# Block-sorted attention and a squared-ReLU MLP in one kernel: turning q, k and x^T on TensorE instead of by transposing transfers

## The chip, the cores and the metric

The kernel runs on one core of a Trainium2 chip. A core has a matrix engine (TensorE, PE in the profile, with its weight loads as PEld), three engines for elementwise work (VectorE or DVE, ScalarE or ACT, GpSimd or POOL), an engine that here only issues transfers (SyncE or SP), and sixteen DMA engines. PE reads from the on-chip memory (SBUF) and writes into PSUM, from where DVE or ACT copies results back. The metric is the device time of one execution in microseconds; the median of several runs counts.

## The reference

Four batches of eight heads, 768 positions, head size 64. A sort matrix of 8x8 for each head is normalised five times by rows and columns and then mixes the eight blocks of 96 positions of k and of v. Each block of q attends to the mixed block of the same number. The result, as x of 3072 tokens by 512, goes through an MLP of width 2048.

```python
    for _ in range(5):
        P = P - np.max(P, axis=-1, keepdims=True)
        P = np.exp(P)
        P = P / (np.sum(P, axis=-1, keepdims=True) + 1e-09)
        P = P / (np.sum(P, axis=-2, keepdims=True) + 1e-09)
    k_sorted = np.einsum('bhij,bhjcd->bhicd', P, k_b).reshape(B, H, S, D)
    v_sorted = np.einsum('bhij,bhjcd->bhicd', P, v_b).reshape(B, H, S, D)
    scores = scale * np.matmul(q_b, k_sb.transpose(0, 1, 2, 4, 3))
    attn = np.exp(scores)
    attn = attn / (np.sum(attn, axis=-1, keepdims=True) + 1e-09)
    # per token, x = attn @ v_sb with the heads side by side
    h = np.maximum(x @ w_in, 0.0)
    return (h * h @ w_out).astype(np.float32)
```

## The kernel before

Work is cut into units of a batch and a pair of heads (`Unit`). A unit needs q turned (head size on the partitions), k sorted and turned, v sorted, the scores (`s_sc`, L684), their exponentials (L704, L713), the product with v (`s_av`, L875), the division (L885, L886), and the turn of the result into x^T (`s_xt`), from which the MLP reads. The MLP (`ffn_unit`) goes in eight groups of 384 tokens: 16 x 4 up matmuls (L997, `hp`) with a relu on ACT (L1005) and a square on DVE (L1008) for each of the 16 tiles, and then three times 16 down matmuls (L1027, `op`; the last tile in two parts, L1055), copied out and stored.

Order. Every step is first recorded as an operation with an engine, a cost and its dependencies. A planner (`Plan.run`) then lays them out. PE has two queues, attention and MLP. Attention operations stand in an order given by the table `DUES`: a number for each step says after how many MLP chunks it is due. `FIRST` is the order written out by hand for the first half of batch 0, with which the kernel starts. `Ring` keeps track of who uses which buffer. Batch 0 is worked off in two halves, before and beside the first MLP groups; batches 1, 2 and 3 are hidden between the MLP groups of the batch before.

How q, k and x^T are turned before the change:

- Batch 0: `s_q` turns q on PE with an identity matrix (L563), `s_sort` and `s_sort2` (L613, L649) multiply k and v by an expanded sort matrix `w_all`, which sorts and turns in one step.
- Batch 1, the first two head pairs: the same steps, in `sort_second`.
- Batch 1, the other two, and batches 2 and 3 (ten units): k is sorted in its own layout by `s_nat` (L769, tiles of 32x32 of PE's array, stage "N"), copied to `kn`, and then `s_turn` (stage "Z") issues a transposing transfer on SP (`k_turn`, L824) into `kx`, which DVE copies into blocks (L829). For q, DVE gathers a pair (`q_pair`, L841) and a second transposing transfer turns it (`q_turn`, L851).
- v of batches 1 to 3 goes by `s_nat` too, and then to DRAM and back in blocks (`v_way`, L793, L799).
- x^T: `s_xt` issues a transposing transfer (L910) for the second half of batch 0, for batches 2 and 3 and for three pairs of batch 1; the rest is turned on PE (L928).

A `gate` on POOL (L390) keeps the early transposing transfers of x^T and the last q load of batch 1 behind a weight load. POOL's `hold` (L1144) lets the loads of batches 2 and 3 start only when x^T of the batch before is there.

While PE has nothing to do before the MLP starts, `fill` (L440) runs matmuls of ones into a PSUM tile. `Ring.idle` chooses the tile: one in which no recorded operation runs during the gap.

The first two pairs of q are loaded in float32 and cast by ACT (L460), after the second and third exponential of the sort matrix.

Of the kernel before, what the change touches and what calls it, by code (L numbers as in the profile page):

```python
# [21 lines left out]
    (0, "K"): (-265.0, -237.0, -495.0, -419.0),  # L22
    (0, "S"): (-232.5, -234.0, -349.0, -310.0),
    (0, "T"): (-184.0, -236.0, -400.0, -291.5),
    (0, "A"): (-135.0, -150.0, -300.0, -111.0),
    (0, "X"): (-58.0, -109.0, -251.5, -80.5),
    (0, "W"): (-267.0,),
    (1, "V"): (-117.0, -62.5),
    (1, "Q"): (-58.5,),
    (1, "N"): (None, -31.0),  # L30
    (1, "Z"): (None, None, 2.5, 48.5),
    (1, "S"): (-45.5, -5.0, 5.0, 50.0),
    (1, "A"): (-27.0, -4.5, 31.5, 51.5),
    (1, "X"): (40.0, 23.5, 37.0, 53.5),
    (2, "L"): (40.0,),
    (2, "N"): (75.5, 79.0),
    (2, "V"): (60.5, 82.5),
    (2, "Z"): (81.0, 82.5, 94.0, 83.5),
    (2, "S"): (86.0, 86.5, 96.0, 93.5),
    (2, "A"): (86.0, 88.0, 99.0, 94.5),  # L40
    (2, "X"): (97.5, 103.0, 103.0, 102.0),
    (3, "L"): (109.0,),
    (3, "N"): (111.5, 130.0),
    (3, "V"): (112.5, 144.0),
    (3, "Z"): (128.5, 139.0, 153.0, 149.0),
    (3, "S"): (144.0, 153.0, 158.0, 153.5),
    (3, "A"): (145.0, 153.5, 159.5, 154.5),
    (3, "X"): (150.5, 170.0, 236.5, 211.5),
# [4 lines left out]
FIRST = ("K0' v0 K1 v1 S0 t0' S1 t1' A0 K2' V2 A1 K3 S2 t2 v3 S3 x1' A2 T3' x0' A3 X2' F0 F1 F3 "  # L53
         "F4 F6 F7 X3")
# [18 lines left out]
class Ring:  # L73


    def __init__(self, n):
        self.users = [[] for _ in range(n)]
        self.all = [[] for _ in range(n)]
        self.turn = -1
        self.pinned = set()  # L80
        self.holders = [None] * n

    def take(self, pin=False):
        assert len(self.pinned) < len(self.users)
        self.turn = (self.turn + 1) % len(self.users)
        while self.turn in self.pinned:
            self.turn = (self.turn + 1) % len(self.users)
        if pin:
            self.pinned.add(self.turn)
        old = self.users[self.turn]  # L90
        self.users[self.turn] = []
        slot = Slot(self.turn)
        self.holders[self.turn] = slot
        return slot, old

    def use(self, slot, *ops):
        assert self.holders[slot] is slot, "taken again before its last use"
        self.users[slot] += ops
        self.all[slot] += ops

    def idle(self, t0, t1):

        for slot, ops in enumerate(self.all):
            if all(op.end <= t0 or op.begin >= t1 for op in ops):
                return slot
# [79 lines left out]
def kernel(  # L185
# [48 lines left out]
    rkx, rkn, rqi, rqz = Ring(3), Ring(4), Ring(4), Ring(6)  # L234
# [43 lines left out]
    kvT_r, et_r, vs_r, qz_r = [], [], [], []  # L278
    for n in range(3):
        sT = const.tile([128, 2, S + 32], BF16, name=f"kvT{n}")  # L280
        for x in (HS, S):
            nc.vector.memset(sT[:, :, x:x + 32], 0.0)
        kvT_r.append(sT)
        qz = const.tile([128, 2, NA, 128], BF16, name=f"qz{n}")
        qz_r.append(qz)
        vs = (qz.rearrange("p h a x -> p (h a x)")[0:96, 0:NB * 2 * 66]
              .rearrange("p (n h x) -> p n h x", n=NB, h=2))
# [13 lines left out]
    kn_r = [const.tile([128, NA, 2, D], BF16, name=f"kn{n}") for n in range(4)]  # L301
    qi_r = [const.tile([128, NA, 2, D], BF16, name=f"qi{n}") for n in range(4)]
    kx_r = []
    for n in range(3):
        kx_r.append(const.tile([128, 128 * NA], BF16, name=f"kx{n}"))
# [8 lines left out]
    w_all = const.tile([128, H + HP, NB, C0], BF16)  # L314
# [22 lines left out]
    def in_tiles(b, t, h0):  # L337
        return b > 1 and t > 0 or b == 1 and t == 2 or b == 1 and t == 1 and h0 == HP
# [44 lines left out]
    def loads_after(deps):  # L383
# [5 lines left out]
        def gate(e):  # L389
            nc.gpsimd.tensor_copy(out=xT[0:1, 0:HP - 1, HS:HS + 1],  # L390
                                  in_=w_out_bf[0:1, NT // 2 - HP + 1:NT // 2, 0:1])

        for t, g in ((2, 0), (2, 1), (1, 0), (0, 0), (1, 1), (0, 1)):
            if t == 0 and g == 1:
                holds["gate"] = plan.add("POOL", 0.1, gate, [landed["w_out", 1]])
                deps = [holds["gate"]]
# [56 lines left out]
    for it in range(5):  # L453
# [3 lines left out]
        if it in (1, 2):  # L457
            def cast(e, g=it - 1):
# [4 lines left out]
                "WAY", (4.3, 5.8)[it - 1], lambda e: None, tail=(4.3, 5.8)[it - 1])]))  # L463
# [67 lines left out]
    class Unit:  # L531


        def __init__(self, b, hp, halves):
            self.b, self.hp, self.halves = b, hp, halves
            self.tiled = in_tiles(b, 1, HP * (hp // 2))
            self.n, self.old = rks.take()
            if self.tiled:
                self.ksT = kvT_r[self.n][:, 0, :]
                self.i0, self.ni, self.full = 0, NB, True  # L540
                return
# [126 lines left out]
    def s_sc(u, due=0):  # L668
# [3 lines left out]
        for hf in u.halves:  # L672
# [4 lines left out]
            def mm(e, hf=hf, st=st, slot=slot):  # L677
                st["p"] = scp = p2[slot]
                if not u.tiled:
                    qT = (tiles["qT", u.b, u.hp].rearrange("p a x -> p (a x)")  # L680
                          .rearrange("p (i q) -> p i q", q=BLK))
                for n in range(NQ):
                    for h in range(2):
# [3 lines left out]
                            rhs=(q_late(u.qz)[64 * h:64 * (h + 1), :,  # L687
                                              C0 * (NQ * hf + n):C0 * (NQ * hf + n + 1)]
                                 if u.tiled else qT[64 * h:64 * (h + 1), NQ * hf + n, :]),
# [5 lines left out]
            if u.tiled:  # L695
                rqz.use(u.qz, pe)
            else:
                rqT.use(qTs[u.b, u.hp], pe)
# [52 lines left out]
    k_nat = {}  # L751

    def s_nat(b, g, t, due):

        if t == 2:
            m, oldm = rvn.take()
        evs = []
        for hp in (2 * g, 2 * g + 1):
            slot, old = r2.take()
            if t == 1:  # L760
                m, oldm = rkn.take()
# [13 lines left out]
            def ev(e, hp=hp, slot=slot, m=m):  # L775
                dst = (vn_r[m][:, :, 2 * (hp % 2):2 * (hp % 2) + 2, 0:D] if t == 2
                       else kn_r[m])
                copy(e, dst, p2[slot][:, :, 0:NA * D].rearrange("p e (a d) -> p a e d", d=D))
# [7 lines left out]
            if t == 1:  # L786
                rkn.use(m, op)
                k_nat[b, hp] = m, op
        if t == 1:
            return  # L790

# [21 lines left out]

    def q_late(z):
        return qz_r[z % 3][:, z // 3, :, :]

    def s_turn(u):

        b, hp = u.b, u.hp
        m, op = k_nat[b, hp]  # L820
        kx, oldx = rkx.take()

        def k_turn(e):
            nc.sync.dma_start_transpose(  # L824
                out=kx_r[kx].rearrange("p (a x) -> p a x", a=NA),
                in_=kn_r[m].rearrange("p a e d -> p (a e d)"))

        def k_blocks(e):
            nc.vector.tensor_copy(out=u.ksT[:, 0:S].rearrange("p (n x) -> p n x", n=NB),  # L829
                                  in_=kx_r[kx].rearrange("p (x n) -> p n x", n=NB))  # L830

        sp = plan.add("SP", 1.4, k_turn, [op, loaded(b)] + oldx)
        k_op = plan.add("WAY", 1.3, lambda e: None, [sp])
        rkn.use(m, k_op)
        u.k_op = plan.add("DVE", 0.87, k_blocks, [k_op] + u.old)
        rkx.use(kx, k_op, u.k_op)

        n, oldi = rqi.take()

        def q_pair(e):  # L840
            nc.vector.tensor_copy(  # L841
                out=qi_r[n].rearrange("p a e d -> p e a d"),
                in_=qkv[b][0][:, 2 * hp:2 * hp + 2, :].rearrange("p e (a d) -> p e a d", d=D))

        qp = plan.add("DVE", 0.4, q_pair, [landed[b, 0, HP * (2 * hp // HP), 0]] + oldi)
        readers[b].append(qp)
        rqi.use(n, qp)
        u.qz, oldz = rqz.take()

        def q_turn(e):  # L850
            nc.sync.dma_start_transpose(  # L851
                out=q_late(u.qz), in_=qi_r[n].rearrange("p a e d -> p (a e d)"))

        sp = plan.add("SP", 1.4, q_turn, [qp, loaded(b)] + oldz + [op for ops in rvs.all for op in ops])
        u.q_op = plan.add("WAY", 1.3, lambda e: None, [sp])
        rqi.use(n, u.q_op)
        rqz.use(u.qz, u.q_op)
# [47 lines left out]
    def s_xt(u, due=0, eng=AD, own=True):  # L905
        early = u.b == 0 and u.halves == (1,) and u.hp < HP - 1
        if early or u.b > 1 or u.b == 1 and u.hp < HP - 1:
            def turn(e):
                t0 = S * u.b + BLK * u.i0
                nc.sync.dma_start_transpose(  # L910
                    out=xT[:, u.hp, t0:t0 + BLK * u.ni].rearrange("p (n q) -> p n q", q=BLK),
                    in_=u.ao.rearrange("p n e d -> p (n e d)"))

            sp = plan.add("SP", 1.4, turn, u.norms + [holds["gate"]] * early)
            op = plan.add("WAY", 6.4 if early else 1.3, lambda e: None, [sp], tail=3.4 if early else None)
            rao.use(u.nao, op)
            for hf in u.halves:
                x_done[u.b, u.hp, hf] = op
            return
# [147 lines left out]
    for hp in range(HP):  # L1067
        qops[hp] = s_q(0, hp, 0, 64, after=exps[2 + (hp + 2) // 3], eng="ACT")
# [18 lines left out]
    for name in FIRST.split():  # L1087
# [21 lines left out]
        else:  # L1109
# [10 lines left out]
              "V": lambda b, g, due: s_nat(b, g, 2, due),  # L1120
# [84 lines left out]
```

## Time and profile before

| What | Before |
|---|---|
| Time, median of 3 runs | 218.05 us (217.73 to 218.27) |
| The profiled execution's own time | 217.95 us |
| Its span, first to last instruction | 216.2 us |
| PE busy | 209.8 us (97%) |
| DVE, ACT, POOL busy | 109.2 (51%), 122.1 (56%), 28.3 us (13%) |
| Granted PE clock | 1.00 throughout |
| Packets of the transfers issued by SP, share of 16 engines' span | 40.1% |
| Packets of the transfers issued by POOL | 36.9% |
| Transposing transfers | 34 (14 xT, 10 kx, 10 qz), 3.6, 3.9, 3.6 us to landing in the median |

The chain of waits follows the work that ended last back from the end; 93% of it is PE. A line of it in order of time has the start, the length, the engine, the tile written and the line of the code, and a count. PE's matmuls overlap, so the length in the chain (from one start to the next) is the cost of a step, not the length of one instruction in the groups.

### The profile page before, as it was taken

The page shows a single profiled execution, that of the slowest core. Times are in us where ns is not written, and L with a number is a line of the kernel's source. Part 1 is how long each engine was busy: PE and PEld are TensorE (multiplying, and loading weights), DVE is VectorE, ACT ScalarE, POOL GpSimd, SP SyncE. Part 2 cuts the span into 40 slices and gives each one's busy share as a digit, 9 for nine tenths or more (in the row PEclk, how much of TensorE's full clock was granted, in tenths as well). Part 3 has the DMA queues.
Part 4 walks back from the last instruction along what each step waited for, and adds up shares of the span by engine and source line. Part 5 has one row for each costly group of instructions (what it writes and reads, how often), then busy time and mean ns, then how long its engine had stood idle before and what let it go on. Part 6 is the DMA issues. An engine that isn't in the chain of part 4 may idle for free.

```text
span 216.2 us, 5062 instructions
## 1 busy us (share of the span) xinstructions
PE 209.8 (97%) x2020; PEld 115.9 (54%) x2036; DVE 109.2 (51%) x297; ACT 122.1 (56%) x251; POOL 28.3 (13%) x53
## 2 busy tenths in 40 slices
PE   8998999999999999999999999999999999999994
PEld 2566675446654565445655455445655465455542
DVE  5777677146795446345875047407775154015300
ACT  4876985248765277347774178318874375137421
POOL 7896230000000700000000420000000000000000
PEclk9999999999999999999999999999999999999999
DMA  6999999999978599199995699497978410120012
GB/s 152 212 203 207 207 207 209 193 226 272 176 164 113 84 238 211 25 192 210 179 186 125 105 201 213 87 207 171 170 204 111 102 47 3 49 97 0 0 52 97
DMA packets 47864, 31.92 MB, mean 148 GB/s; under 512 B 27296, under 2 KB 42912, under 8 KB 47840
## 3 DMA queue, kind: packets, MB, share of 16 engines
q1 hardware_dynamic: 35616, 18.35, 40.1%
q0 software_dynamic: 12224, 13.24, 36.9%
q8 instruction: 16, 0.26, 0.5%
q14 instruction: 8, 0.07, 0.1%
HBM read 29.70 MB, written 8.72 MB: 178 GB/s over the span
## 4 chain that ended last, share of the span: by engine, by line
PE 93%; DVE 2%; ACT 2%; issue 1%; DVEq 0%
PE hp L997 37%; PE op L1027 36%; PE p L875 4%; PE p L440 4%; PE p L684 3%; PE p L769 2%; PE op L1055 2%; PE qtp L563 2%; DVE ao L886 1%; PE vbp L733 1%; PE p L649 1%; DVE h L1008 1%; ACT h L1005 1%; PE xtp L928 1%; PE hp L955 0%
## 5 line engine op out<-in xcount | busy, mean ns | idle before, releaser
L997 PE MATMUL hp<-xT,w_in_bf 128*128 128x384 bf16 x506 | 87.6, 326 | 0.0
L1027 PE MATMUL op<-w_out_bf,h 128*128 128x512 bf16 x352 | 83.3, 379 | 0.9 <-issue 0.2
L1008 DVE TENSOR_TENSOR h<-h 128x384 bf16<-128x384 bf16 x128 | 43.9, 355 | 56.2 <-ACT h L1005 55.7
L1005 ACT ACTIVATE h<-hp 128x384 bf16<-128x384 f32 x128 | 61.7, 495 | 17.7 <-PE hp L997 14.9
L997 PEld LDWEIGHTS <-w_in_bf 128*128 128x128 bf16 x506 | 47.7, 98 | 32.2 <-issue 1.1
L1027 PEld LDWEIGHTS <-h 128*128 128x128 bf16 x368 | 33.9, 98 | 37.9 <-issue 1.0
L248 ACT COPY ob<-op 128x512 f32<-128x512 f32 (+2 forms) x25 | 14.2, 568 | 49.1 <-PE op L1027 46.6
L713 ACT ACTIVATE et<-p 96x384 bf16<-96x384 f32 x48 | 19.9, 488 | 6.4 <-PE p L684 6.4
L886 DVE TENSOR_TENSOR ao<-p,rec 96x512 bf16<-96x512 f32 x32 | 22.0, 686 | 1.1
L875 PEld LDWEIGHTS <-et 96*128 96x128 bf16 x256 | 11.2, 97 | 5.5 <-issue 0.7
L885 DVE RECIPROCAL rec<-p 96x8 f32<-96x8 f32 x32 | 6.4, 201 | 11.1 <-PE p L875 10.5
L1144 POOL COPY held<-xT 1x3 bf16<-1x3 bf16 (+1 forms) x2 | 0.4, 183 | 85.0 <-DMA xT<-ao 85.0
L440 PE MATMUL p<-ones 128*128 128x512 bf16 (+1 forms) x28 | 9.2, 460 | 1.1 <-DVE ones L274 1.1
L875 PE MATMUL p<-vblk,et 96*128 96x65 bf16 x192 | 9.4, 193 | 0.1
L250 DVE CAST vn<-p 128x768 bf16<-128x768 f32 x6 | 5.7, 958 | 7.3 <-PE p L769 7.2
L250 DVE CAST kn<-p 128x768 bf16<-128x768 f32 x5 | 4.8, 958 | 9.1 <-PE p L769 9.1
L684 PEld LDWEIGHTS <-kvT 64*128 64x128 bf16 x256 | 6.2, 94 | 5.5 <-issue 3.6
L829 DVE COPY kvT<-kx 128x768 bf16<-128x768 bf16 x10 | 8.5, 850 | 0.0
L248 ACT CAST vn<-p 128x768 bf16<-128x768 f32 x6 | 4.8, 798 | 5.8 <-PE p L769 5.8
L324 POOL DMA_DIRECT2D kb<-in_k_dram x10 | 6.5, 648 | 4.1 <-DMA w_in_bf<-in_moe_w_in_dram 2.0
L248 ACT CAST kn<-p 128x768 bf16<-128x768 f32 x5 | 4.0, 806 | 4.7 <-PE p L769 4.7
L324 POOL DMA_DIRECT2D vb<-in_v_dram x10 | 6.3, 633 | 2.3 <-DMA w_in_bf<-in_moe_w_in_dram 2.1
(81 smaller groups left out, 118.8 us busy)
## 6 DMA issues: line engine op xcount, KB each, us to landing
out_dram<-ob SPq DMA_DIRECT2D x23, 256.0 KB, 3.4
v_way<-vn SPq DMA_DIRECT2D x6, 396.0 KB, 5.1
vblk<-v_way SPq DMA_DIRECT2D x6, 396.0 KB, 4.3
vb<-in_v_dram POOLq DMA_DIRECT2D x6, 384.0 KB, 11.7
kb<-in_k_dram POOLq DMA_DIRECT2D x6, 384.0 KB, 10.4
qb<-in_q_dram POOLq DMA_DIRECT2D x6, 384.0 KB, 13.1
w_in_bf<-in_moe_w_in_dram POOLq DMA_DIRECT2D x4, 512.0 KB, 10.4
w_out_bf<-in_moe_w_out_dram POOLq DMA_DIRECT2D x4, 512.0 KB, 15.7
```

Of the source, the lines that this page charges most:

```text
L248: nc.scalar.copy(out=out, in_=in_)
L250: nc.vector.tensor_copy(out=out, in_=in_)
L324: nc.gpsimd.dma_start(out=dst, in_=src)
L440: nc.tensor.matmul(out=p2[slot][:, 0, 0:128 * r].rearrange("p (r x) -> p r x", r=r), lhsT=ones, rhs=ones[:, None, :].to_broadcast([128, r, ...
L684: nc.tensor.matmul(out=scp[:, h, BLK * n:BLK * (n + 1)], lhsT=u.ksT[64 * h:64 * (h + 1), HS * hf + BLK * n:HS * hf + BLK * n + 128], rhs=( ...
L713: nc.scalar.activation(out=et[:, h, 0:HS].rearrange("p (n c a) -> p n c a", c=C0, a=NA), in_=st["p"][0:96, h, 0:HS].rearrange("p (n a c) - ...
L875: nc.tensor.matmul(out=oup[:, h, 66 * n:66 * n + D + 1], lhsT=et_r[u.et[hf]][:, h, BLK * n:BLK * n + 128], rhs=(u.vs[:, NQ * hf + n, h, 0: ...
L886: nc.vector.tensor_tensor(out=u.ao[:, n0:n0 + NQ, :, :].rearrange("p n e d -> p e n d"), in0=ov[:, :, :, 0:D], in1=rec[:, :, :, None].to_b ...
L997: nc.tensor.matmul(out=t["hp", nt][:, 0:HS], lhsT=w_in_bf[:, kc, 128 * nt:128 * (nt + 1)], rhs=xT[:, kc, t0:t0 + HS], start=(kc == 0), sto ...
L1005: nc.scalar.activation(out=t["h1", nt], in_=t["hp", nt][:, 0:HS], func=AF.Relu)
L1008: nc.vector.tensor_tensor(out=t["h2"][:, nt, :], in0=t["h1", nt], in1=t["h1", nt], op=ALU.mult)
L1027: nc.tensor.matmul(out=t["op", mt], lhsT=t["h2"][:, nt, 128 * mt:128 * (mt + 1)], rhs=w_out_bf[:, nt, :], start=(nt == 0), stop=(nt == NT ...
```

## The change

1. Transposing transfers are gone, and with them `s_turn`, `q_late`, the tiles `kn`, `qi`, `kx` and `qz` (the sorted v of batch 0 gets tiles of its own, `vs`), stages "N" and "Z", and the gate. Batches 1 to 3 use `s_q` on PE for q (stage "Q", `turn_q`) and `s_sort` with `w_all` for k (stage "J", `sort_k`), and `s_xt` turns every x^T on PE. `w_all` is kept for all 32 heads; POOL builds the part of batches 2 and 3 after their loads. k of all batches is loaded by positions, not in tiles.
2. `Ring.idle` counts a PSUM tile as taken from the first operation of a holding to its last, so that a filler never writes into a tile that holds something unread.
3. The second cast of q follows the fourth exponential instead of the third.
4. `FIRST` and all of `DUES` are new, and with them the order of the work on every engine.

```diff
-FIRST = ("K0' v0 K1 v1 S0 t0' S1 t1' A0 K2' V2 A1 K3 S2 t2 v3 S3 x1' A2 T3' x0' A3 X2' F0 F1 F3 "
-         "F4 F6 F7 X3")
+FIRST = ("K0 v0 k1 S0 v1 t0' K2' S1 t1' A0 K3 V2 V3' A1 S2 t2' x0 x1' S3 A2 T3 F0 X2 A3 F3 F1 "
+         "F6 F4 F7 x3")
...
-        for slot, ops in enumerate(self.all):
-            if all(op.end <= t0 or op.begin >= t1 for op in ops):
+        for slot, holds in enumerate(self.all):
+            if all(max(op.end for op in ops) <= t0 or min(op.begin for op in ops) >= t1
+                   for ops in holds if ops):
                 return slot
...
     def in_tiles(b, t, h0):
-        return b > 1 and t > 0 or b == 1 and t == 2 or b == 1 and t == 1 and h0 == HP
+        return b > 0 and t == 2
...
-            if t == 0 and g == 1:
-                holds["gate"] = plan.add("POOL", 0.1, gate, [landed["w_out", 1]])
-                deps = [holds["gate"]]
...
-        if it in (1, 2):
-            def cast(e, g=it - 1):
+        if it in (1, 3):
+            def cast(e, g=it // 2):
...
-        early = u.b == 0 and u.halves == (1,) and u.hp < HP - 1
-        if early or u.b > 1 or u.b == 1 and u.hp < HP - 1:
-            def turn(e):
-                t0 = S * u.b + BLK * u.i0
-                nc.sync.dma_start_transpose(
-                    out=xT[:, u.hp, t0:t0 + BLK * u.ni].rearrange("p (n q) -> p n q", q=BLK),
-                    in_=u.ao.rearrange("p n e d -> p (n e d)"))
...
-    def turn(b, hp, due):
-        u = units[b, hp] = Unit(b, hp, (0, 1))
-        s_turn(u)
+    def sort_k(b, hp, due):
+        u = units[b, hp] = Unit(b, hp, (0, 1))
+        if b == 1 and hp % 2 == 0:
+            for h0 in (2 * hp, 2 * hp + 2):
+                build_w(H + h0, 2, pt, x_done[0, 2, 1])
+        u.k_op = s_sort(u, 1, due)
+        u.q_op = late_q[b, hp]
+
+    late_q = {}
+
+    def turn_q(b, hp, due):
+        late_q[b, hp] = s_q(b, hp, 0, 128, due)
...
-        holds[b] = plan.add("POOL", 0.1, hold, [x_done[b - 1, x, 0] for x in range(HP - (b == 2))])
+        holds[b] = plan.add("POOL", 0.1, hold, [x_done[b - 1, x, 1] for x in range(HP - (b == 2))])
         landed["last"] = plan.add("DMA", 4.5, lambda e: None, [holds[b]])
         for g in range(2):
             for t in (1, 2, 0):
                 load(b, t, HP * g, HP)
-
+        for h0 in range(0, H, 4):
+            build_w(H * b + h0, 4, pt, holds[b], eng="POOL")
```

## The prediction

> **What bounds the kernel now.** I read the page's first part, then the windows, the waits of TensorE and the chain in order of time, which prices the steps. The page first: busy time by engine, and a group of its fifth part that a change of transfers must be held against.
>
> ```profile
> PE 209.8 (97%) x2020; PEld 115.9 (54%) x2036; DVE 109.2 (51%) x297; ACT 122.1 (56%) x251; POOL 28.3 (13%) x53
> PEclk9999999999999999999999999999999999999999
> L997 PE MATMUL hp<-xT,w_in_bf 128*128 128x384 bf16 x506 | 87.6, 326 | 0.0
> ```
>
> TensorE (PE) is busy 97% at full clock. Busy alone does not say that it is at its peak, so next the chain in time (start, length, what, how many). The stretch from 47.48 holds q and k work of the old kind, 73.51 a turn of x^T, 88.99 a k sort in tiles, 61.23 scores in two halves, and 171.44 plain up-projection with hardly any transfer beside it.
>
> ```profile
> 47.48 1.30 PE hp L997 x8
> 48.78 0.46 PE qtp L563 x12
> 49.24 0.67 PE p L613 x24
> 49.91 0.76 PE hp L997 x4
> 50.67 0.46 PE qtp L563 x12
> 51.12 0.45 PE p L684 x16
> 51.57 1.41 PE hp L997 x8
> 52.97 0.49 PE p L769 x16
> ...
> 61.23 0.28 PE p L684 x8
> ...
> 73.51 0.34 PE xtp L928 x8
> 73.85 1.73 PE op L1027 x8
> 75.58 8.45 PE hp L997 x52
> ...
> 88.99 0.31 PE p L769 x16
> ...
> 171.44 9.76 PE hp L997 x60
> ```
>
> One up matmul takes 1.30/8 = 0.1625 us, one down matmul 1.73/8 = 0.2165. The whole MLP is 512 x 0.1625 + 368 x 0.2165 + 3.5 (the last tile) = 166.4 us. From 20.0, where it starts, to 213.0, where its last matmul ends, are 193.0 us; the other 26.6 are attention matmuls. The windows, summed, confirm it: from 20 to 192 us PE is busy 170.85 of 172.00 us. So **1.15 us** is all that PE waits in that stretch. Its own list of waits says the same:
>
> ```profile
> PE p L440 <- DVE ones L274: 1.1, 1, 1.1
> PE p L875 <- ACT qz L248: 0.5, 1, 0.5
> PE p L684 <- DVE ao L886: 0.3, 1, 0.3
> PE op L1027 <- issue: 0.2, 1, 0.2
> ```
>
> None is for a transfer. The 34 transposing transfers (landing after 3.6 to 3.9 us in the median) are waited for by POOL and DVE, in time that PE does not feel. Work added to PE after 20 us therefore lengthens the run one for one, and there is next to nothing to win back.
>
> **The change part by part.** The instruction order of the new kernel gives the counts.
>
> *k.* Removed: 5 sorts in tiles (80 matmuls, L769), 0.49 + 4 x 0.31 = 1.73 us. An MLP matmul after another array layout starts late: 0.76 instead of 0.65 for four, 1.41 instead of 1.30 for eight, so 0.11 for each exit; 5 exits, 0.55. Together **-2.3**. Added: 10 sorts as in L613, 0.67/2 = 0.335 each, 3.35.
>
> *q.* Added: 10 turns as in L563, 0.46 each (entry into the layout included), 4.6. Turns and sorts stand in 14 stretches of the new order, two of them a sort alone (its entry, about 0.1 each, 0.2 in all). Eleven more exits to MLP work than before, 1.2. q and k added: **+9.35**.
>
> *x^T.* 11 turns more of eight (0.34) and 3 of four (0.17 to 0.21 in the chain): 3.74 + 0.55 = **+4.3**. They need no change of layout (73.85: 1.73, the plain price).
>
> *Scores.* The new order has four pairs of half units less: a pair costs 2 x (0.28 + 0.10 of exit) against 0.45 + 0.11, so 4 x -0.2 = **-0.8**.
>
> Sum on PE: -2.3 + 9.35 + 4.3 - 0.8 = **+10.6 us**.
>
> [...]
>
> *Transfers and SP.* 34 issues of about 1.25 us leave SP's queue, and it keeps the outputs and the six v round trips. PE waited for none of them: 0. [...]
>
> *VectorE and ScalarE.* DVE loses the copies of kx (8.5), of qi (3.2) and five kn (4.8), and gains 9 qT (0.558 each), 9 xT (0.557), 3 short xT (0.35), 2 kvT (0.956) and 2 w_all (0.42), 13.8 in all: 2.7 less, on an engine 51% busy. ACT loses kn (4.0) and gains 8 kvT (0.80), 2 xT and 1 qT (no row; between 0.58, its 96x512 bf16 copy, and 0.80): 4.8 more, to 127. In sum both are covered by PE. Single hand-overs are not: x^T and q share one PSUM tile, and in batch 3 two q turns stand four down matmuls (0.87) apart, just the 0.56 copy and two hand-overs of 0.1 to 0.2. The last x^T has the same 0.87 before the up-projection that reads it. Some twelve such places, each 0 (planned to fit) to 0.2: I take 0.4, ends **0 and 2.4**. Nearest is before's own 1.15 us of idle for as many tight places.
>
> *POOL.* The gate (0.19) goes; four w_all builds of 512 elements come in (before: 256 in 0.66, so about 1.3 each), queued behind the six loads of their batch. The hold for batch 2 ran at 71.3, its loads were issued by 75.4; the builds end near 78, and the sort that reads them comes after up matmul 192, past 86. Cover: eight us of MLP. 0.
>
> *Second q cast.* It ran 6.48 to 7.31 and the exponentials came exactly 1.76 us apart (2.50, 4.26, 6.02, 7.78, 9.54), so it held up nothing; one exponential later it runs 8.04 to 8.87, free again before 9.54. In its place two q copies stand before the exponential due at 7.78; the q load that one needs lands by about 7.1. 0, at most 0.15.
>
> *Fillers and first order.* 30 instead of 28, in time in which PE waits. In the start ACT carries the same five sort copies, four exponentials and a v copy from 13.0 to 19.6, nearly without gaps, so the first MLP matmuls come where they did. I take 0; ends **-0.5** (all ACT's gaps there) and **+0.7** (one copy more of 0.48 and a hand-over before the last attention product).
>
> Total 10.6 + 0.4 = 11.0. The sum is made against the profiled execution: 217.95 us (span 216.2, 1.75 around it), 0.1 under the median 218.05 of the runs. So **229.0 us**, its own range 227.3 to 231.
>
> **The rivals.**
>
> *A transfer arrives late for batch 1, and PE stands.* q of the second half was issued at 31.64 and landed at 52.2; the new order needs it in its second q turn, at 47.48 + 0.55 (three x^T turns) + 0.91 (q, k, exit) + 3.9 (24 up) = 52.8. The sorted v came back near 57.7 (issue 53.37, 4.3 to land) and is needed near 58.6 instead of 59.26. For it: less than one us of room, and k's second half now comes in 768-byte pieces. Against it: the three early transposing transfers and their gate no longer stand among these loads. Two to three us of waiting would give 231 to 232.
>
> *ScalarE bounds the second up-projection.* 16 relus x 0.495 + 12 exponentials x 0.488 + two or three k copies x 0.80 + a q copy are 15.4 to 17.0 us; PE's work in that stretch is 14.9. Some of it spills into the down-projection that follows, where ACT is idle: 0.5 to 2 us, 229.5 to 231.
>
> *Not slower: the transposing traffic slowed the matmuls, and without it they run faster.* Place: all MLP matmuls; it decides from 10.4 us on 166, that is 0.1523 instead of 0.1625 each. Against it: 52 up matmuls in 8.45 us at 75.58 among transfers are 0.1625, 60 in 9.76 at 171.44, DMA share 0.13, are 0.1627. There is nothing to gain; this would give 218.
>
> *The layout changes cost nothing* (the entries and exits fold into the next weight load): 9.35 falls to 6.7, the k removal to -1.55, the scores to 0: +9.45, and with the start's -0.5 and no hand-over 217.95 + 8.95 = 226.9. The rows of 0.76 and 1.41 speak against it.
>
> **How the numbers follow.** Forecast (227.3 to 231) 0.68; late transfer 0.13; ScalarE beyond its share 0.07; free layout changes 0.09; not slower 0.03. The range goes from 226.5 (the last rival, less 0.4 of before's idle 1.15) to 232.5 (10.6 + 2.4 + 0.7 + 0.8 of waiting). About 0.3%, 0.65 us, can be told from no change; faster 0.02, same 0.01, slower 0.97.
>
> **What would show it.** Right: from 20 us to the end PE still busy over 98%, up matmuls at 0.1625, q turns near 0.46, x^T turns near 0.34 and k sorts near 0.335 in the chain, no transposing transfer, the unbroken MLP work from near 20 us. Wrong: PE idle of several us near 52 or 58 us (late transfer), hp waiting for relu between 50 and 62 (ScalarE), up matmuls under 0.155 (traffic), or a start shifted by a us.

## The result, and the profile after

The changed kernel takes **229.75 us** in the median of four runs (228.96 to 231.74), the kernel before 218.13 us on the same chip (217.73 to 218.27). The ratio is 1.0549, with a 95% interval of 1.0491 to 1.0607: 11.6 us slower. The profiled execution is the slowest of the four, 231.74 us (span 230.0); the other profiles below show where such executions differ from one another. Medians here and below are over all executions, while the ratios leave out those in a slower state, told by a time over 1.5% above the fastest of the same kernel.

The page of the kernel after, by engine, by transfer queue, and the group of the up matmuls:

```profile
PE 222.7 (97%) x2298; PEld 127.1 (55%) x2298; DVE 107.3 (47%) x297; ACT 127.3 (55%) x257; POOL 33.8 (15%) x56
PEclk9799999999999999999999999999999999999999
q1 hardware_dynamic: 9568, 11.95, 16.3%
L899 PE MATMUL hp<-xT,w_in_bf 128*128 128x384 bf16 x506 | 87.8, 326 | 0.0
```

PE has 278 matmuls more in its records and 12.9 us more of busy time. Sixteen of the 278 are records that the trace of before lacks, at the line of the down matmuls, which has 352 matmuls but 368 weight loads there and 368 of both after:

```profile
L1027 PE MATMUL op<-w_out_bf,h 128*128 128x512 bf16 x352 | 83.3, 379 | 0.9 <-issue 0.2
L1027 PEld LDWEIGHTS <-h 128*128 128x128 bf16 x368 | 33.9, 98 | 37.9 <-issue 1.0
```

So 262 matmuls were added. The queue q1, which held the transposing transfers, has gone from 35616 packets (40.1%) to 9568 (16.3%). One up matmul still lasts 326 ns. The 7 in the second place of the clock's row is new.

To see where the time went I cut both chains at the same two steps: the first half of the sort matrix laid out for w_all (`pt_ps`), and the 48 matmuls that sort the second half of batch 0 (L649 before, L629 after), with which the unbroken MLP stretch begins. The kernel before, its chain in order of time (start, length, what, how many):

```profile
11.94 0.31 PE pt_ps L474 x8
...
21.44 0.88 PE p L649 x48
...
213.04 0.27 ACT ob L248
```

The kernel after, the same view:

```profile
1.24 6.10 DMA qb<-in_q_dram
7.38 0.57 PE qtp L543 x24
7.95 4.28 PE p L425 x12
...
14.50 0.31 PE pt_ps L459 x8
...
25.03 0.88 PE p L629 x48
...
51.77 0.46 PE qtp L543 x12
52.23 0.34 PE p L593 x12
52.56 4.01 PE hp L899 x24
...
73.43 0.34 PE xtp L830 x8
...
185.06 10.40 PE hp L899 x64
...
226.66 0.27 ACT ob L248
```

| Part of the chain | Before | After | Difference |
|---|---|---|---|
| Start to `pt_ps` | 11.94 | 14.50 | +2.56 |
| `pt_ps` to the 48 sorts | 9.50 | 10.53 | +1.03 |
| 48 sorts to the last copy | 191.60 | 201.63 | **+10.03** |

In the last part the steps have the prices that were read from before: a q turn 0.46, a k sort 0.34, a turn of x^T 0.34, 64 up matmuls 10.40, that is 0.1625 each. Its difference, summed over the chain by tile: q turns +4.60 (twelve instead of two), k sorts with `w_all` +3.65, x^T +4.47, sorts in tiles -1.50, scores -0.48, products with v -0.72. (From 108.5 to 112.4 us before's chain runs over other engines and leaves out 16 score matmuls and 8 products; they are counted here at 0.28 and 0.25 us for eight.) That is 10.02, so all the rest, the MLP and its exits included, comes out even.

The first part is another matter. Its chain begins with a q load that took 6.10 us, and PE's list of waits after (engine, tile and line, what it waited for: total, times, longest) has a first line that before did not have:

```profile
PE qtp L543 <- DMA qb<-in_q_dram: 1.6, 1, 1.6
PE p L425 <- DVE ones L274: 1.1, 1, 1.1
PE xtp L830 <- DVE ao L802: 0.7, 1, 0.7
```

The timeline of PE in the start of the kernel after (start, length, what; in brackets the idle time before it and what ended it):

```profile
7.38 0.57 PE L543 MATMUL qtp<-ident,qb 64*64 64x64 bf16 x24 [1.65 <-DMA qb<-in_q_dram]
7.88 4.34 PE L425 MATMUL p<-ones 128*128 128x512 bf16 x12
```

And its windows (busy time and instructions of PE, its weight loads, DVE, ACT and POOL, then the granted clock, DMA share and GB/s), with one window from the middle of the run:

```profile
5.50:7.40 1.90, 0.25 (x14) 0.14 (x10) 1.37 (x8) 0.87 (x3) 1.81 (x3) 1.00 1.28 231
...
9.00:10.50 1.50, 1.50 (x5) 0.47 (x4) 1.04 (x6) 0.77 (x3) 1.37 (x3) 0.50 1.29 199
10.50:12.20 1.70, 1.70 (x7) 0.50 (x7) 1.46 (x8) 0.00 (x0) 1.38 (x6) 0.55 1.30 197
...
50.00:62.00 12.00, 12.00 (x148) 7.21 (x147) 5.53 (x15) 8.95 (x20) 0.00 (x0) 1.00 0.45 125
```

PE stands 1.65 us for the q load. A little over a us after it is back at work its granted clock falls to half, and the twelve fillers, which take 12 x 0.217 = 2.6 us at full clock (four take 0.86 in this kernel's chain from 12.81 on, and the window from 12.20 to 13.70 reads 1.00), take 4.3. Fillers stand in PE's order ahead of real work: the sort matrix was ready at 12.16 (11.90 before) and PE came to it at 14.43. By these numbers some 1.7 of the 2.56 us are the clock and the rest the wait, an estimate. From 50 to 62 us, where a late transfer or ScalarE could have held PE, it is busy without a gap.

### The profile page after: what moved, and what is told of

It reads as the page before. It is cut to its first block, busy times and chain, and to the rows that moved or that the text cites. A ratio compares the mean times of both kernels' runs of the same rounds, so it can differ in the third digit from the quotient of the medians.

```text
span 230.0 us, 5531 instructions
## 1 busy us (share of the span) xinstructions
PE 222.7 (97%) x2298; PEld 127.1 (55%) x2298; DVE 107.3 (47%) x297; ACT 127.3 (55%) x257; POOL 33.8 (15%) x56
## 3 DMA queue, kind: packets, MB, share of 16 engines
q1 hardware_dynamic: 9568, 11.95, 16.3%
## 4 chain that ended last, share of the span: by engine, by line
PE 94%; DMA 3%; DVE 1%; issue 1%; ACT 0%; DVEq 0%; POOLq 0%
PE hp L899 36%; PE op L929 35%; PE p L791 4%; PE qtp L543 3%; PE p L663 3%; DMA qb<-in_q_dram 3%; PE xtp L830 3%; PE p L425 2%; PE p L593 2%; PE op L957 2%; PE tp L593 1%; PE p L738 1%; PE p L629 1%; PE vbp L707 1%; DVE ao L802 1%
## 5 line engine op out<-in xcount | busy, mean ns | idle before, releaser
L929 PE MATMUL op<-w_out_bf,h 128*128 128x512 bf16 x368 | 85.6, 379 | 0.0
L910 DVE TENSOR_TENSOR h<-h 128x384 bf16<-128x384 bf16 x128 | 44.5, 356 | 51.0 <-ACT h L907 50.8
L248 ACT CAST kvT<-p 128x768 bf16<-128x768 f32 x11 | 8.8, 801 | 9.3 <-PE p L593 7.4
L425 PE MATMUL p<-ones 128*128 128x512 bf16 (+1 forms) x30 | 10.8, 508 | 1.1 <-DVE ones L274 1.1
L250 DVE COPY qT<-qtp 128x768 bf16<-128x768 bf16 x11 | 6.1, 556 | 12.0 <-PE qtp L543 12.0
L250 DVE COPY xT<-xtp 128x768 bf16<-128x768 bf16 (+1 forms) x16 | 7.6, 479 | 8.2 <-PE xtp L830 7.9
L543 PE MATMUL qtp<-ident,qb 128*64 128x128 bf16 (+1 forms) x240 | 8.7, 212 | 1.6 <-DMA qb<-in_q_dram 1.6
L543 PEld LDWEIGHTS <-qb 128*64 128x64 bf16 (+1 forms) x240 | 6.2, 109 | 7.0 <-issue 4.1
L830 PE MATMUL xtp<-ident,ao 96*128 96x96 bf16 x128 | 8.8, 206 | 0.8 <-DVE ao L802 0.7
L830 PEld LDWEIGHTS <-ao 96*128 96x128 bf16 x128 | 7.1, 97 | 4.3 <-DVE ao L802 1.6
## 6 DMA issues: line engine op xcount, KB each, us to landing
vb<-in_v_dram POOLq DMA_DIRECT2D x6, 384.0 KB, 11.6
```

The source lines that it names most:

```text
L248: nc.scalar.copy(out=out, in_=in_)
L250: nc.vector.tensor_copy(out=out, in_=in_)
L425: nc.tensor.matmul(out=p2[slot][:, 0, 0:128 * r].rearrange("p (r x) -> p r x", r=r), lhsT=ones, rhs=ones[:, None, :].to_broadcast([128, r, ...
L543: nc.tensor.transpose(out=t["p"][64 * h:64 * (h + 1), a, :], in_=qb[p0:p1, 2 * hp + h, D * a:D * (a + 1)], identity=ident[p0:p1, p0:p1])
L830: nc.tensor.transpose(out=xtp[:, n, :], in_=u.ao[:, n, :, :].rearrange("p e d -> p (e d)"), identity=ident[0:96, 0:96])
L910: nc.vector.tensor_tensor(out=t["h2"][:, nt, :], in0=t["h1", nt], in1=t["h1", nt], op=ALU.mult)
```

## The experiments

Two questions were open. Is the +10.03 of the long stretch really PE's added work, one for one, or is traffic or the new order in it? And what is the start's part: the new first order, the new place of the second q cast, or the clock? The first theory: PE-bound throughout, plus a start in which PE idles for the q load and loses its clock. Its rivals: the transposing traffic had its own price (so that part of the gain was eaten elsewhere), the new first order alone costs the start, or the late load costs what it costs whatever the clock does. Every ratio below is to the kernel before on the same chip, with its 95% interval.

**The changed kernel again.** No edit. The two kernels with the casts of before and the one with the warm wait ran on the same chip.

> The changed kernel once more, for the spread of its start. Theory: PE idles while the second q turn waits for its load; where that wait is over a microsecond the granted clock falls to half, the twelve fillers behind it take 4.3 us instead of 2.6, and the spread of the sort matrix (pt_ps) starts up to 2.6 us later. So times from 229.0 (no wait) to 231.7 (as in the profile), the later the spread the longer the time, and everything from the batch-0 sorts (L629) to the end 201.6 us in each profile. Rival: the spread over runs lies in the MLP stretch, and the start is the same each time.

Median 231.12 us of six (228.82 to 233.47), ratio 1.0570 (1.0531 to 1.0608). In its profile (233.47) the load landed 7.6 us after its issue. PE's timeline in the start:

```profile
8.87 0.85 PE L543 MATMUL qtp<-ident,qb 64*64 64x64 bf16 x24 [2.90 <-DMA qb<-in_q_dram]
9.65 4.47 PE L425 MATMUL p<-ones 128*128 128x512 bf16 x12
```

The wait is 2.90 us, the fillers again take 0.37 each, and `pt_ps` comes at 16.40, 4.5 us later than before. About 2 of the 4.5 us come by ACT: a q copy that waits for this turn stands ahead of the fourth exponential, which ran at 9.81 (7.78 before), so the sort matrix itself was ready only at 13.89 (11.90 before). The fillers hold it up for the rest. The stretch from the 48 sorts on is 201.63, the same to the hundredth. So these two executions of the changed kernel differ in their start alone.

The granted clock in this trace reads 1.00 throughout. The single fillers behind the wait say otherwise (count: shortest, median and longest in ns, first and last start); the kernel after, the repeated run, and a run below in which the clock stayed full:

```profile
L425 PE MATMUL p<-ones x12: 374/634/634, 7.9 to 11.8; 128*128 128x512 bf16 x11, 128*128 128x256 bf16 x1
L425 PE MATMUL p<-ones x12: 273/634/634, 9.7 to 13.8; 128*128 128x512 bf16 x11, 128*128 128x256 bf16 x1
L432 PE MATMUL p<-ones x5: 379/379/390, 10.3 to 11.2; 128*128 128x512 bf16 x5
```

In the repeated run a filler lasts 634 ns, as in the profile of after while its granted clock read 0.50.

**The casts of before in the changed kernel.** The second cast goes back behind the third exponential, and the q turns of the start back to the order of before.

```diff
-        if it in (1, 3):
-            def cast(e, g=it // 2):
+        if it in (1, 2):
+            def cast(e, g=it - 1):
...
-                "WAY", (4.3, 7.8)[it // 2], lambda e: None, tail=(4.3, 7.8)[it // 2])]))
+                "WAY", (4.3, 5.8)[it - 1], lambda e: None, tail=(4.3, 5.8)[it - 1])]))
...
-    for hp, it in ((0, 2), (2, 2), (3, 3), (1, 4)):
-        qops[hp] = s_q(0, hp, 0, 64, after=exps[it], eng="ACT")
+    for hp in range(HP):
+        qops[hp] = s_q(0, hp, 0, 64, after=exps[2 + (hp + 2) // 3], eng="ACT")
```

> The changed kernel with the cast of before (after the second and third exponential) and q turned in the order 0, 1, 2, 3 again; FIRST and DUES stay new. Theory: the load has until the cast of the second pair has ended (near 7.3 us), PE has fillers in between, the clock stays at 1.00 and the spread of the sort matrix starts near 11.9 us: 229.0 in every run, 0.7 under the changed kernel's median. Rival (the start costs nothing, the 11.6 us are all in the MLP stretch): 229.7 as before.

Median 229.27 us, 1.0517 (1.0500 to 1.0535). Five of its six runs lie within 0.5 us, from 228.92 to 229.42; the sixth took 235.68 and was not profiled. In the profile `pt_ps` is back at 11.91, the 48 sorts come at 22.21 instead of 21.44, and the stretch is 201.63. So the delay before `pt_ps` goes with part 3 of the change and the new order of the q turns (pairs 0, 2, 3, 1 instead of 0, 1, 2, 3, which the list of the change does not name); the two were undone together, and which of them does it was not separated. The +0.8 between `pt_ps` and the sorts stays.

**The same and the first order of before.**

```diff
-FIRST = ("K0 v0 k1 S0 v1 t0' K2' S1 t1' A0 K3 V2 V3' A1 S2 t2' x0 x1' S3 A2 T3 F0 X2 A3 F3 F1 "
-         "F6 F4 F7 x3")
+FIRST = ("K0' v0 K1 v1 S0 t0' S1 t1' A0 K2' V2 A1 K3 S2 t2 v3 S3 x1' A2 T3' x0' A3 X2' F0 F1 F3 "
+         "F4 F6 F7 X3")
```

> The changed kernel with the cast, the order of q and FIRST all of before. Theory: besides the wait, the new FIRST costs 1.0 us between the spread of the sort matrix and the batch-0 sorts (10.5 us against 9.5 in the two profiles); with both undone 228.0, just the 10.0 us that the MLP stretch gained on PE. Rival (FIRST was late only because the clock had been low): 229.0, as with the cast alone.

Median 229.42 us (229.16 to 231.27), 1.0537 (1.0508 to 1.0567): nothing won against the run above, where 1.0 us was expected. In the profile `pt_ps` to the sorts is 9.51, as before the change, but the stretch after it is 202.36, 0.73 longer. What the old first order wins in the start it loses later. This execution, the slowest of the six, also happened to get its second float load late, by the cast on ACT, so the old casts do not shut such waits out:

```profile
8.87 0.83 ACT L445 CAST qb<-xT 128x768 bf16<-128x768 f32 x1 [2.73 <-DMA xT<-in_q_dram]
```

PE idled 2.72 us there, and yet the four fillers behind it took 0.93 us, as four did in the profile of after from 12.74 on at a clock of 1.00. Single ones lasted 379 ns. So an idle time of this length does not always slow what follows.

**The first order of before alone**, in the changed kernel with its new casts; the diff is the one just shown.

> The changed kernel with FIRST of before alone; the cast and the order of q stay new. Theory: 1.0 us less than the changed kernel run by run, 228.0 where the load is in time and up to 230.7 where it is not. Rival (FIRST costs nothing once the clock is full): no difference.

Median 229.95 us of four (228.81 to 234.42), 1.0525 (1.0474 to 1.0577), not to be told from the changed kernel, where 1.0 us less was expected. `pt_ps` to the sorts is 10.22, with a wait of 0.5 us on PE in it whose cause the profile does not show; the stretch is again 202.36. Its chain shows the place of most of the loss:

```profile
48.47 0.19 PE xtp L830 x4
48.67 0.37 DVE xT L250
49.09 0.53 PE qtp L543 x12
```

With this order the last x^T turn of batch 0 stands directly ahead of the first q turn of batch 1. They share one PSUM tile, and PE waits for the copy between them.

**A warm wait.** Matmuls of ones for 1.7 us between the first and the second q turn of the changed kernel, so that PE does not idle while it waits for the load.

```diff
+        if hp == 0:
+            plan.add("PE", 1.7, lambda e: fill(1.7, 1))
```

> The changed kernel with 1.7 us of matmuls of ones put between the first q turn and the second, where PE waited for the load (the planner then puts fewer behind them). Theory (idle PE lowers the clock): the clock stays at 1.00 though the load comes when it comes, the spread of the sort matrix starts at 11.9 to 12.3 us, 229.0 to 229.4 in every run. Rival (the late load itself delays, through the q copy that stands before an exponential on ScalarE): the start is as late as in the changed kernel whenever the load is, up to 2.6 us.

Median 229.31 us, 1.0533 (1.0500 to 1.0565); five of six within 228.81 and 229.91, the sixth 231.26. On the same chip the unedited kernel took 231.12, so this and the old casts are each about 1.8 us lower in the median; by the ratios it is 0.8 and 1.2 us, and the intervals overlap, so neither gain is clear of the spread. In the profiled execution the load came in time anyway, so the profile does not show the mechanism at work; the next pair does.

**The load made late, without and with work in the wait.** Two transfers of 192 KB into tiles that nobody reads go ahead of the q loads, so that the load is late in every execution. The second kernel also gets 3.2 us of ones matmuls in the wait.

```diff
+    idle = [const.tile([128, 2, NA * D], BF16, name=f"idle{n}") for n in range(2)]
+
+    def ahead(e):
+        for n in range(2):
+            nc.gpsimd.dma_start(out=idle[n], in_=v_r[0, :, 2 * n:2 * n + 2, :])
+
+    plan.add("POOL", 0.0, ahead)
```

Second kernel, in addition:

```diff
+        if hp == 0:
+            plan.add("PE", 1.7, lambda e: fill(3.2, 1))
```

> The changed kernel with two loads of 192 KB into spare tiles issued ahead of the q loads, so that q comes about 2 to 3 us later in every run; the planned order is the same. It is to reproduce the late start on purpose: PE waits 2 to 4 us before the second q turn, the twelve fillers behind it take over 4 us instead of 2.66, the spread of the sort matrix starts at 16 to 17 us, and the time is 232 to 235.

> The same late loads, but with 3.2 us of matmuls of ones in the place where PE waits. The exponentials still wait for the q copy that stands before them on ScalarE, so the last transposed part of the sort matrix is as late as in the run without them (near 14 us). Theory (idle PE lowers its clock): the fillers behind the second turn run at 0.217 us each and the spread follows the sort matrix within 0.4 us, at 13.5 to 14.5: some 2 us less than without. Rival (the fillers were slow for another reason, such as the loads under way): they take 0.36 us each here too, and the spread is as late.

Late alone: 234.52 us (234.46, 234.58), 1.0754 (1.0723 to 1.0786). Late with work: 231.45 us (231.35, 231.55), 1.0614 (1.0583 to 1.0645). PE's timeline of the first:

```profile
9.84 0.85 PE L550 MATMUL qtp<-ident,qb 64*64 64x64 bf16 x24 [4.20 <-DMA qb<-in_q_dram]
10.62 4.57 PE L432 MATMUL p<-ones 128*128 128x512 bf16 x12
```

Of the second:

```profile
5.65 2.98 PE L432 MATMUL p<-ones 128*128 128x512 bf16 x13
9.84 0.56 PE L550 MATMUL qtp<-ident,qb 64*64 64x64 bf16 x24 [1.21 <-DMA qb<-in_q_dram]
10.34 1.25 PE L432 MATMUL p<-ones 128*128 128x512 bf16 x5
...
17.34 0.38 PE L600 MATMUL tp<-w_all,kb 128*64 128x64 bf16 x12 [0.62 <-POOL w_all L478]
```

The windows of the first, from 10 to 12 us (columns as above):

```profile
10.00:12.00 2.00, 2.00 (x28) 1.11 (x27) 0.82 (x4) 1.59 (x4) 1.40 (x2) 0.50 1.32 202
```

And of the second:

```profile
10.00:12.00 2.00, 2.00 (x60) 1.18 (x58) 0.00 (x0) 1.74 (x5) 1.40 (x2) 1.00 1.29 194
```

The turn that reads the load starts at the same 9.84 in both, with the same loads under way, and the clock stays at 1.00 where it was 0.50; the fillers behind the wait take 0.25 each instead of 0.38. So idle time can lower the clock, and where it does the wait costs twice: once as a wait, and once more through the clock of what follows.

How much of the 3.07 us is the clock is less sure, for the two kernels differ in more than the ones matmuls. The planner puts only five fillers behind the wait instead of twelve, and the fourth exponential ahead of the waiting q copy (at 7.57 instead of 10.79), so that the sort matrix is ready at 14.02 instead of 14.79. `pt_ps` comes at 13.78 instead of 17.46, 3.68 earlier. By the rows, the turn (0.28 shorter) and twelve fillers at full price (2.6 instead of 4.5) would give 2.2 of that, an estimate; the rest then goes to the different order.

What remains of the late load (231.45 against some 229.3) comes by ACT and POOL. In the second kernel a q copy and the cast stand at 10.26 and 10.63, ahead of the last exponential, which runs at 11.73, and `pt_ps` follows the sort matrix directly. Later PE waits 0.62 us for a part of `w_all` that POOL builds (the last line above); POOL had waited 0.3 us twice for the q loads before it issued the next ones.

**Traffic put back.** Two transposing transfers for each unit of batches 1 to 3, 24 in all, into tiles that nobody reads.

```diff
+        if u.b > 0:
+            for n in range(2):
+                def turn(e, n=n):
+                    nc.sync.dma_start_transpose(
+                        out=spare[n], in_=u.ao.rearrange("p n e d -> p (n e d)"))
+
+                sp = plan.add("SP", 1.4, turn, u.norms)
+                rao.use(u.nao, plan.add("WAY", 1.3, lambda e: None, [sp]))
```

> The changed kernel with two transposing transfers more for each unit of batches 1 to 3 (24 in all) of the attention result into a spare tile that nobody reads; PE's work is the same. Theory (transposing transfers were hidden and did not slow matmuls): up matmuls stay at 0.1625 us and the time within 0.7 of the changed kernel. Rival (the traffic slows the matmuls, so that its removal gave something back): with 24 of 34 transfers back, matmuls over 0.165 us and several us longer.

Median 229.39 us (228.30 to 230.44), 1.0516 (1.0466 to 1.0567). The page's line for the queue, and then the chain of this kernel:

```profile
q1 hardware_dynamic: 28768, 16.68, 31.8%
```

```profile
22.71 0.88 PE p L630 x48
...
203.52 10.40 PE hp L908 x64
...
224.35 0.27 ACT ob L248
```

The queue carries 31.8% instead of 16.3%, 64 up matmuls still take 10.40 us, and the stretch is 201.64. These 24 transposing transfers cost the stretch 0.01 us: they did not slow the matmuls, and nothing was to be had by taking them away.

**x^T turned twice.** The twelve turns of batches 1 to 3 are issued twice.

```diff
-            for n in range(u.ni):
+            for n in [*range(u.ni)] * (2 if u.b > 0 else 1):
```

> The changed kernel with every x^T turn of batches 1 to 3 done twice into the same PSUM tile: 12 x 8 transposes more. Theory (PE has no idle time, so its work adds one for one): 12 x 0.33 = 3.9 us over the changed kernel, 3.6 to 4.4. Rival (part of the added turns hides in waits of PE): under 2 us.

Median 232.79 us, 1.0671 (1.0642 to 1.0701). In the chain x^T goes from 4.98 to 9.22 us (+4.24), the stretch from 201.63 to 205.87 (+4.23).

```profile
22.75 0.88 PE p L629 x48
...
228.62 0.27 ACT ob L248
```

PE's added work lengthens the stretch one for one; nothing absorbs it.

**The three turns, one at a time, in the kernel before.** x^T alone, with earlier due times for the turns of batch 3:

```diff
-    (3, "X"): (150.5, 170.0, 236.5, 211.5),
+    (3, "X"): (150.5, 162.0, 168.0, 165.0),
...
-        if early or u.b > 1 or u.b == 1 and u.hp < HP - 1:
+        if False:
```

> The kernel before with every x^T turned on PE (as after), q and k still by transposing transfers; three due times of batch 3's x^T are set to 162, 168 and 165 so that they do not stand in one block. Theory: 11 x 0.34 + 3 x 0.18 = 4.3 us over before, 4.0 to 5.5 as the order was not tuned for it. Rival (x^T turns hide in waits): under 2 us.

q alone:

```diff
-    def s_turn(u):
+    def s_turn(u, due):
...
-        u.q_op = plan.add("WAY", 1.3, lambda e: None, [sp])
-        rqi.use(n, u.q_op)
-        rqz.use(u.qz, u.q_op)
+        u.q_op = s_q(b, hp, 0, 128, due)
```

> The kernel before with the q of its ten late units turned on PE instead of by transposing transfers, k and x^T as before. Theory: 10 x 0.46 + seven exits x 0.11 = 5.4 us over before, up to 7 where the order, not tuned for it, makes PE wait. Rival (layout changes cost nothing): 3.4.

k alone:

```diff
-    w_all = const.tile([128, H + HP, NB, C0], BF16)
+    w_all = const.tile([128, NH, NB, C0], BF16)
...
-        k_op = plan.add("WAY", 1.3, lambda e: None, [sp])
-        rkn.use(m, k_op)
-        u.k_op = plan.add("DVE", 0.87, k_blocks, [k_op] + u.old)
-        rkx.use(kx, k_op, u.k_op)
+        u.k_op = s_sort(u, 1, due)
```

> The kernel before with the k of its ten late units sorted and turned on PE in one step instead of sorted in tiles and turned by a transfer; q and x^T as before. Theory: 10 x 0.335 + eight entries and exits x 0.24 - 2.3 = 3.0 us over before, 2.5 to 4.5. Rival (k in tiles was as dear): 1 or less.

| Alone in the kernel before | Median us | Ratio (95%) | Stretch against 191.60 |
|---|---|---|---|
| x^T | 225.63 | 1.0336 (1.0312 to 1.0359) | +6.6 |
| q | 223.63 | 1.0247 (1.0229 to 1.0265) | +5.8 |
| k | 223.08 | 1.0227 (1.0206 to 1.0248) | +5.05 |

Every part is slower by itself. q cost about what was expected (5.4), x^T and k some two us more than theirs (4.3 and 3.0), outside the ranges given. A part of that shows as waits, 0.9 us in one place each. x^T alone, PE's waits:

```profile
PE xtp L928 <- ACT qT L248: 0.9, 1, 0.9
```

k alone:

```profile
PE p L681 <- DMA qz<-qi: 0.9, 1, 0.9
```

In the order of before a turn meets the shared PSUM tile while a q copy is still to be read from it, or scores come up before the transposing transfer of q has landed; where the rest went was not followed. The three alone sum to +17.5 us in the stretch, the whole change is +10.03. If they simply add, doing all three in the new order saves about 7 us (17.5 - 10.0). Likely places are that q and k share entries, that scores and products with v are done in pairs, and that turns stand where their tile is free; the all-together change in the old order was not run.

## Why the prediction was right or wrong

*PE bounds it, and added work counts one for one.* Right, and shown: the +10.03 is made up of chain steps at the prices of before, and a doubled x^T adds 4.23 us for 4.24 of work. One reading behind it was off, on the safe side. Of the 1.15 us that PE seemed idle between 20 and 192 us, 0.9 lie at the line of the down matmuls, where the trace lacks 16 records; and the waits of 0.5 and 0.3 in the list come before 20 us. PE waited even less than was said, and the 1.15 was no measure for hand-overs.

*The terms.* Measured in the stretch against predicted: the added q turns 4.60 against 4.6; x^T 4.47 against 4.3; k sorts 3.65 against 3.35 and the 0.2 of lone entries; the removed tile sorts -1.50 against -1.73 without their exits. Scores and exits together were foretold at -0.8 - 0.55 + 1.2 = -0.15 and came out near -0.5, if the exits are even; they are not measured by themselves. One term was missing: the new order also pairs products with v, -0.7. With it the sum on PE falls from 10.6 to about the 10.0 that was measured.

*Hand-over stalls, 0.4.* Mis-sized: PE had no wait worth listing after the start. That such places can cost is shown by the runs of x^T and k alone (0.9 each, once) and by the old first order (0.73); in the new order they cost nothing.

*Transfers and SP, 0.* Right: 24 transposing transfers added to the changed kernel moved its stretch by 0.01 us. No part of the change was faster alone: x^T +6.6, q +5.8 and k +5.05 us in the stretch.

*VectorE, ScalarE and POOL covered.* Right for the MLP stretch: from 50 to 62 us PE was busy 12.00 of 12.00. The late transfer for batch 1 did not show, nor did ScalarE bound the second up-projection. POOL did show in the start: in three profiles (traffic put back, x^T turned twice, the late load with work) PE waited 0.6 us for a part of `w_all` that POOL builds. Part 2 of the change was not run by itself.

*First order, 0 (-0.5 to +0.7).* Too low: `pt_ps` to the sorts is +1.03 in the profile of after, +0.80 with the old casts and about +1.5 in the three profiles with the wait for POOL, which is 0.6 of it. The rest buys a better hand-over later: with the old casts the old first order wins the start back (9.51), with the new ones a part of it (10.22), and both times the stretch is 0.73 longer, most of it at 48.7 us.

*"Second q cast: 0, at most 0.15".* This step failed. It looked at ACT's queue and took the load to land by about 7.1; it landed at 7.3 in the profile of after and at 8.8 in the repeated run, and the exponential due at 7.78 ran at 8.17 and 9.81. It did not look at PE's queue. The new order of the q turns puts a turn that reads a freshly loaded pair directly behind the first, with no filler between them, and the load lands 4.7 to 7.6 us after its issue, by the execution. Where it is late PE idles, the clock may fall to half (0.50 after 1.65 us of idle in the profile of after), and the twelve fillers, laid out for full clock, hold up the sort matrix. That is 2.56 us in the profile of after and 4.5 in the one of the repeated run. Where the load is early it is next to nothing: with the traffic put back and with x^T turned twice, which leave the start alone, the load took 5.0 and 5.1 us and PE came to `pt_ps` at 11.7, as early as before. The prediction's own sign against it, a start shifted by a us, did show.

So the predicted 229.0 met 229.75, but in part by luck, because errors cancelled: the stretch took 1.0 less than 10.6 + 0.4, the first order 0.8 to 1.5 more than 0, and the late load the rest. The low end of the range, 227.3, does not follow from the terms either: 217.95 + 10.6 - 0.5 is 228.05.

None of the runs beat the kernel before. Of the changes to the start none is clear of the others; the old casts have the lowest median, 229.27, with five of six runs within 0.5 us.

## What to carry to other kernels

Where the profile shows one engine at 97% and no wait for the transfers, work moved onto that engine can be priced by rows of the chain, here to 0.6 us in 10; moving it cost its full price here, however untidy the transfers looked. But look at every place where that engine's order changes, the fill time at the start too: a step that only moves can put a wait on a load whose landing varies (here 4.7 to 7.6 us after its issue), and filler work laid out for full clock can then stand in the way at half clock (here 4.3 us instead of 2.6). Do not judge a part by its cost in an order that was not made for it: the three parts, each alone in the old order, sum to 7 us more than all of them together in the new one.

## What the runs showed of the hardware

- The windows show PE's granted clock at half in two profiles, each time with an idle time of PE early in the run. In the profile of after it dropped once, after 1.65 us of idle: the windows' 0.89 from 7.40 to 9.00 and 0.55 from 10.50 to 12.20 put the half clock from about 8.65 to 12.03, 3.4 us. With the late load, where PE idled for 4.20 us, 0.94 from 5.50 to 8.00 and 0.91 from 14.00 to 17.00 put it from about 7.7 to 14.5, 6.8 us. With most of the same wait filled by matmuls of ones the clock stayed at 1.00.
- What sets the half clock off is not shown. 1.65 us of idle were once enough; 2.72 us another time, with the old casts and the old first order, were not: single fillers lasted 379 ns behind them. No run here explains that. "Over a microsecond" in the expectation for the repeated run was the author's estimate, and no run shows an idle time that decides it.
- The granted clock in the records does not show every such drop: in the repeated run it read 1.00 while single fillers lasted 634 ns, as they did under 0.50 in the profile of after, against 379 at 1.00. That the clock was half there too is inferred from these durations.
- The same 192 KB q load, issued at 1.25 us, landed after 4.7 us in the profile of the kernel before, 6.1 in that of after and 7.6 in the repeated run. What decides it stays open.
